# An attention and two-layer MoE kernel: w_in fetched up front, GpSimd without elementwise work behind the gating, column maxima turned at later steps

## The chip, the cores and the metric

One core of one Trainium2 chip runs the kernel. The metric is the device time of one execution in microseconds (us); the time given for a kernel is the median of its runs.

## The reference

The inputs are q, k, v of shape (4, 8, 576, 64), s of shape (4, 8, 576), and for each of two layers w_in (512 x 2048) and w_out (2048 x 512) in float64. Cut to what matters:

```
scores = q @ k^T / sqrt(64) + min(cum_k - cum_q, 0)   # causal; cum = cumsum(max(s, 0))
x  = softmax(scores) @ v                # 4 x 8 x 576 x 64 -> 2304 tokens x 512
h  = x @ w1_in;  g = h * tanh(log(1 + exp(h)));       x = g @ w1_out
h2 = x @ w2_in;  g2 = h2 * sigmoid(1.702 * h2);     out = g2 @ w2_out
```

## The kernel before

**Stages.** Attention runs over 4 batches, 8 heads and blocks of 128 rows (576 is 4.5 blocks). The first layer's first matmul runs between its steps, for units of 256 tokens: `first_layer` makes `h` out of `xh` (x, split in a high and a low part) and a tile `w` of w_in, and stores it to DRAM (`h_d`). Then the *gating* (`act`) loads pieces `hg` of it, applies Mish on ScalarE (`z`) and splits the result into `gh` (high) and `gl` (low). The second matmul of the first layer (`acc<-gh,w`, `acc<-gl,w`) goes over 5 *spans* of tokens, four of 512 and one of 256, with 16 *steps* each; a step is one block of 128 rows of w_out and has 12 matmuls. The accumulators `acc` of a span of 512 tokens hold four PSUM banks, and spans use two sets of four in turn. After a span, `out1` copies the banks out, takes maxima (`mx`) and stores x to DRAM (`x_d`). The second layer makes `h` out of x in fp16 halves (`x16`) and `w2i` (`first2`), `z<-h,sg` behind a sigmoid, combinations `s` of its four quarters (`combos`), and `p<-w2h,gl` and the like with seven products in place of eight (`second2`). Every product of split numbers is three matmuls: high by high, high by low, low by high (`mm3`).

**Weights.** They arrive as float64. `fetch_w` loads a piece as 128x1024 int32 (512 KB) into a tile `wst`; `turn_w` converts it: a scaling on ScalarE, a shift (TENSOR_SCALAR) and one or two SCALAR_TENSOR_TENSOR of 128x512 on VectorE, then the high half `th` and the low half `tl_`. In the first layer's w_out, both halves are made on GpSimd. w_in has 16 pieces, `fetch_a` fetches them in order from a list `fq`, and `bg_a` turns the next; `first_layer` calls both as it goes. A dependency lets a fetch start only behind the last transpose of the opening (`weights behind transposes`).

**The second layer's weights** are scaled first, during the first layer's second matmul, as *jobs*, one at a step: `out_pass1` (16 times) converts a piece of w2_out, takes its maxima (`wom`) and stores it, `in_pass` (16 times) converts a piece of w2_in and takes `wim`, `in_split` makes `w2i`. `out_pass2` then reads w2_out back in pairs (`w2f`), makes four differences `w2d` of 128x256 on GpSimd, and splits them into `w2h` and `w2l`.

**Maxima across partitions.** `across(col, then, wait)` copies a column to 128x128 (`bc`) on VectorE; after `wait` calls of `soon_step`, one to a step and one at each end of a span, TensorE transposes it into a bank of the set not in use (`acc<-ident,bc`), and VectorE reduces it (`spx<-acc` or `gsc<-acc`). Seven columns go this way: the scale of w2_out (`out_scale`, wait 14), of w2_in (`in_scale`, wait 7), and the maximum of x in each of the five spans (wait 14 for the first three; the last two are taken at the second layer's start).

**Order.** The Tile framework's scheduler places instructions on the engines' queues by priority and dependencies; in the opening (`nc.mode = "strict"`) every engine keeps the order in which the program emits. The w_in pieces of the first layer and `h_d` go by SP's queue, q and k of later blocks by GpSimd's (`load_group`, `k_load`), with a doubling copy of each on ScalarE. All instructions are recorded at one line (L77, in `Lane.run`), so tiles' names tell them apart.

Of the kernel before, what the change touches and what calls it, by code (L numbers as in the profile page):

```python
# [29 lines left out]
SOON = 7  # L30
# [4 lines left out]
PTB = 5  # L35
WAH = 1
LAG0 = 2
NEAR = 26
FA = 3
XH = 3  # L40
# [50 lines left out]
def attention_moe_moe_kernel(  # L91
# [107 lines left out]

    def k_load(i, g):  # L200
        t = pp.tile([128, HG, 2, D], F32, tag="kraw", name="kraw", bufs=3)
        nc.gpsimd.dma_start(out=t[:, :, 0, :], in_=rows(k, 0, i, g))
        held(nc.scalar.activation(out=t[:, :, 1, :], in_=t[:, :, 0, :], func=AF.Copy))
        raw[0, i, g] = t

    def load_group(b, i, g):
        n = min(128, S - 128 * i)
        r = []
        for src, nm in ((k, "kraw"), (q, "qraw"), (v, "vraw")):
            if nm == "vraw" and b == 0:  # L210
                v_load(i, g, nc.gpsimd)
                continue
            w = 1 if nm == "vraw" else 2
            t = pp.tile([128, HG, w, D], F32, tag=nm, name=nm, bufs=2 if nm == "qraw" else 3)
            held(nc.gpsimd.dma_start(out=t[:n, :, 0, :], in_=rows(src, b, i, g)))
            if w == 2:
                held(nc.scalar.activation(out=t[:n, :, 1, :], in_=t[:n, :, 0, :], func=AF.Copy))
            else:
                t = t[:, :, 0, :]
            r.append(t)  # L220
        raw[b, i, g] = r
# [525 lines left out]
    def fetch_w(stage, lay, m, kind):  # L747
        if stage:
            rt = stage.tile([128, 1024], F32, tag="wst", name="wst", bufs=NRAW)
        else:  # L750
            rt = tmp_pair(F32, "wst")
        if wide:
            rv = rt.bitcast(I32)
            r = rv.rearrange("p (f two) -> p f two", two=2)
            src = (w1_in, w2_in, w1_out, w2_out)[lay + 2 * (kind == "out")].bitcast(I32)
        else:
            rv = r = rt[:, 0:DM]
            src = (w1_in, w2_in, w1_out, w2_out)[lay + 2 * (kind == "out")]
        if kind == "in":
            n = src.shape[1] // NF  # L760
            ld = nc.sync.dma_start(
                out=rv.rearrange("p (c f) -> p c f", c=KC),
                in_=src[:, m * n:(m + 1) * n].rearrange("(c p) f -> p c f", p=128),
            )
            if lay == 0 and last_pt[0] is not None:
                tc.add_manual_dep(ld.ins, last_pt[0].ins.name, order, reason="weights behind transposes")
        else:
            nc.sync.dma_start(out=rv, in_=src[m * 128:(m + 1) * 128, :])
        fetched[lay, m, kind] = r

    def turn_w(pool, lay, m, kind):
# [19 lines left out]
        if not sided:  # L791
            nc.vector.scalar_tensor_tensor(
                out=yi, in0=yi, scalar=-(2 ** 31), in1=zi, op0=ALU.bitwise_and, op1=ALU.bitwise_or
            )
        if lay == 0 and kind == "out":
            nc.gpsimd.tensor_scalar(out=th, in0=y, scalar1=1.0, scalar2=0.0, op0=ALU.mult, op1=ALU.add)
        else:
            nc.scalar.activation(out=th, in_=y, func=AF.Copy)
        nc.gpsimd.tensor_tensor(out=tl_, in0=y, in1=th, op=ALU.subtract)

# [187 lines left out]
    def act(i):  # L988
# [5 lines left out]
        for e in range(2):  # L994
# [61 lines left out]
    def across(col, then, wait=SOON):  # L1056
# [150 lines left out]
    def out_pass2(j):  # L1207
# [19 lines left out]
    for i, (u, t0, W, m0, n) in enumerate(groups1):  # L1227
# [24 lines left out]
        if m0 + n == NF:  # L1252
# [3 lines left out]
            def out1(e, acc=acc, k_=k_, mx=mx, u=u, t0=t0, W=W):  # L1256
# [167 lines left out]
```

## Time and profile before

| | |
|---|---|
| median of 3 runs | 1035.53 us (1034.38 to 1039.54) |
| profiled execution | 1039.73 us, of which the span is 1038.0 |
| mean granted clock of TensorE | 0.978 |
| busy: TensorE | 985.0 us (95%) |
| busy: VectorE | 689.9 us (66%) |
| busy: ScalarE | 544.9 us (52%) |
| busy: GpSimd | 387.2 us (37%) |
| DMA | 143.17 MB, mean 138 GB/s |

The shares of busy time are means over stages. In the page's slices of 25.95 us, VectorE has nine tenths or eight in those from 415 to 571 us, and three to six tenths in the last quarter; TensorE has nine tenths in nearly all. The granted clock is a share of 2.4 GHz: 0.50 is the lower level, 1.2 GHz. In the rows below, PE is TensorE, DVE VectorE, ACT ScalarE, POOL GpSimd. A row of a timeline gives start and duration in us, engine, operation, out<-in, count, and in brackets the idle time before it and what ended that. A row of waits gives who waited for whom, the total, how often, and the longest. A row of windows gives a stretch, its length, each engine's busy time (x instructions), the granted clock, the share of the DMA engines and GB/s. A row of groups gives the shape, the count, busy us in total, the mean of one in ns, and the idle time before them with what ended it.

### The profile page before, as it was taken

How to read it: one execution, taken by the hardware profiler on the slowest of the kernel's cores; microseconds unless marked ns; L12 is line 12 of the kernel's file. 1: busy time of each engine (PE TensorE's matmuls, PEld its weight loads, DVE VectorE, ACT ScalarE, POOL GpSimd, SP SyncE). 2: the span in 40 equal slices, each digit the busy share in tenths (PEclk: the TensorE clock that was granted, in tenths of full speed). 3: DMA queues.
4: the chain of work that ended last, by engine and by line, in shares of the span. 5: the costliest groups of instructions: out<-in, count | busy, mean ns of one | idle time of the engine just before them, and what ended most of it. 6: DMA issues, size and time to landing. Idle time of an engine off the chain costs nothing.

```text
span 1038.0 us, 20212 instructions
## 1 busy us (share of the span) xinstructions
PE 985.0 (95%) x7966; PEld 872.4 (84%) x7970; DVE 689.9 (66%) x1257; ACT 544.9 (52%) x1054; POOL 387.2 (37%) x414
## 2 busy tenths in 40 slices
PE   6799999989989899999996989999999999999997
PEld 5688798879979789998885868988888888888886
DVE  6478677755565775799998984985653653653553
ACT  4476577766665885365655564553433433333331
POOL 2544442243123311586321315575343442342431
PEclk9789999999999999999998999999999999999999
DMA  6458359997699978779996552600110100000000
GB/s 174 107 146 246 102 133 167 221 234 164 138 212 220 171 158 182 271 268 347 339 339 211 201 203 81 203 22 1 41 42 1 39 24 1 21 19 3 21 9 34
DMA packets 153775, 143.17 MB, mean 138 GB/s; under 512 B 91216, under 2 KB 122448, under 8 KB 153680
## 3 DMA queue, kind: packets, MB, share of 16 engines
q1 hardware_dynamic: 147456, 124.05, 43.9%
q0 software_dynamic: 6224, 17.83, 6.7%
q8 instruction: 62, 1.02, 0.4%
q14 instruction: 33, 0.27, 0.1%
HBM read 89.61 MB, written 32.58 MB: 118 GB/s over the span
## 4 chain that ended last, share of the span: by engine, by line
PE 48%; DVE 11%; DMA 10%; issue 3%; ACT 3%; POOL 2%; SPq 1%; DVEq 0%; ACTq 0%; POOLq 0%
PE h L77 24%; PE p L77 16%; DVE wst L77 5%; PE acc L77 4%; PE s L77 2%; DMA wst<-in_moe_w_out_dram 2%; DMA pt<-hl 2%; PE o L77 1%; DMA wst<-in_moe_w_in_dram 1%; DVE gl L77 1%; DMA vraw<-in_v_dram 1%; DMA h_d<-hs 1%; POOL w L77 1%; POOL w2d L77 1%; DMA w2f<-w_d 1%
## 5 line engine op out<-in xcount | busy, mean ns | idle before, releaser
L77 PE MATMUL h<-x,w2i 128*128 128x256 f16 x1728 | 200.0, 273 | 0.0
L77 PE MATMUL acc<-gh,w 128*128 128x512 f32 (+1 forms) x640 | 185.0, 374 | 13.5 <-DVE spx L77 13.5
L77 PE MATMUL h<-xh,w 128*128 128x256 f32 x1344 | 196.6, 295 | 1.1 <-ACT xh L77 0.7
L77 PEld LDWEIGHTS <-w2i 128*128 128x128 f16 x1728 | 169.0, 98 | 19.6
L77 PEld LDWEIGHTS h<-xh,w 128*128 128x128 f32 x1344 | 172.8, 195 | 4.1 <-ACT xh L77 1.1
L77 PEld LDWEIGHTS acc<-gh,w 128*128 128x128 f32 x640 | 117.9, 191 | 35.8 <-DVE spx L77 14.4
L77 PE MATMUL p<-w2h,gl 128*128 128x256 f16 x504 | 135.9, 273 | 1.1 <-DVE gl L77 1.1
L77 PE MATMUL p<-w2l,gh 128*128 128x256 f16 x504 | 136.0, 273 | 0.0
L77 PE MATMUL p<-w2h,gh 128*128 128x256 f16 x504 | 133.4, 273 | 1.1 <-ACT gh L77 0.9
L77 POOL TENSOR_TENSOR s<-z 128x256 f32<-128x256 f32 x72 | 54.7, 780 | 201.8 <-DVE z L77 201.8
L77 PE MATMUL acc<-gl,w 128*128 128x512 f32 (+1 forms) x320 | 119.2, 373 | 0.0
L77 PEld LDWEIGHTS <-gh 128*128 128x128 f16 x1008 | 98.5, 98 | 12.9 <-ACT gh L77 1.2
L77 ACT ACTIVATE sg<-h,spx 128x512 f32<-128x512 f32 x72 | 48.7, 680 | 105.0 <-PE h L77 105.0
L77 DVE TENSOR_TENSOR gl<-z,gh 128x768 f16<-128x768 f32 (+1 forms) x54 | 77.1, 1428 | 34.5 <-ACT gh L77 21.9
L77 DVE SCALAR_TENSOR_TENSOR wst<-wst 128x512 int32<-128x512 int32 x96 | 91.1, 958 | 10.0 <-ACT wst L77 6.6
L77 DVE SCALAR_TENSOR_TENSOR z<-h,sg 128x512 f32<-128x512 f32 x72 | 49.3, 687 | 68.8 <-ACT sg L77 68.7
L77 POOL TENSOR_TENSOR gl<-z,gh 128x1024 fp32r<-128x1024 f32 x18 | 51.0, 2832 | 116.9 <-ACT gh L77 103.8
L77 DVE TENSOR_TENSOR gl<-s,gh 128x1024 f16<-128x1024 f32 x36 | 44.2, 1228 | 68.5 <-ACT gh L77 68.5
L77 ACT ACTIVATE gh<-z 128x1024 fp32r<-128x1024 f32 (+1 forms) x72 | 67.9, 947 | 33.8 <-DVE z L77 29.4
L77 PE MATMUL s<-kw,qw 128*128 128x288 f32 (+4 forms) x352 | 81.8, 339 | 2.4 <-DVE kw L77 2.2
L77 ACT ACTIVATE gh<-s 128x1024 f16<-128x1024 f32 x36 | 38.0, 1057 | 81.7 <-POOL s L77 81.7
L77 ACT ACTIVATE P<-P,mx 128x128 f32<-128x128 f32 (+4 forms) x108 | 62.7, 582 | 19.9 <-DVE mx L77 19.5
(146 smaller groups left out, 1765.2 us busy)
## 6 DMA issues: line engine op xcount, KB each, us to landing
h_d<-hs SPq DMA_DIRECT2D x36, 512.0 KB, 4.4
hg<-h_d SPq DMA_DIRECT2D x36, 512.0 KB, 6.4
wst<-in_moe_w_in_dram SPq DMA_DIRECT2D x32, 512.0 KB, 5.3
wst<-in_moe_w_out_dram SPq DMA_DIRECT2D x32, 512.0 KB, 5.4
ck<-cum_d SPq DMA_DIRECT2D x6, 768.0 KB, 7.8
x_d<-x SPq DMA_DIRECT2D x18, 256.0 KB, 5.2
out_dram<-o SPq DMA_DIRECT2D x9, 512.0 KB, 2.8
kraw<-in_k_dram POOLq DMA_DIRECT2D x32, 128.0 KB, 4.1
```

What stands on the lines that cost most here:

```text
L77: r = f(*a, **kw)
```

## The change

(1) All 16 pieces of w_in are fetched in the opening, into slots of the pool that holds their converted form (the last into a slot of another pool); the dependency behind the transposes is gone, and `first_layer` fetches no more. `load_group` and `k_load` of the third block of rows are issued earlier, without their doubling copies, which follow later (`twice`). `bg_a` is called more often in the opening, and `WAH` goes from 1 to 3. (2) `act` makes both `gl` on VectorE; the low half of w_out is made on VectorE and the high half on ScalarE; the differences `w2d` are made on VectorE. GpSimd keeps the low halves of w_in and `combos`. (3) `across` counts absolute steps where `wait` is over 7: 57 for `out_scale`, 66 for `in_scale`, and 59, 60, 65, 999, 999 for the five spans.

```diff
-WAH = 1
+WAH = 3
...
-FA = 3
...
+    def twice(t, n=128):
+        held(nc.scalar.activation(out=t[:n, :, 1, :], in_=t[:n, :, 0, :], func=AF.Copy))
...
-            rt = tmp_pair(F32, "wst")
+            rt = (wa_p if m < NF - 1 else mo_a).tile([128, 1024], F32, tag="w" if m < NF - 1 else "hs", name="wst")
...
-            if lay == 0 and last_pt[0] is not None:
-                tc.add_manual_dep(ld.ins, last_pt[0].ins.name, order, reason="weights behind transposes")
...
-        if lay == 0 and kind == "out":
-            nc.gpsimd.tensor_scalar(out=th, in0=y, scalar1=1.0, scalar2=0.0, op0=ALU.mult, op1=ALU.add)
-        else:
-            nc.scalar.activation(out=th, in_=y, func=AF.Copy)
-        nc.gpsimd.tensor_tensor(out=tl_, in0=y, in1=th, op=ALU.subtract)
+        nc.scalar.activation(out=th, in_=y, func=AF.Copy)
+        (nc.gpsimd if kind == "in" else nc.vector).tensor_tensor(out=tl_, in0=y, in1=th, op=ALU.subtract)
...
-    for _ in range(FA):
+    while fq:
         fetch_a()
...
     score(3)
+    load_group(0, 2, 0, False)
+    for i_ in range(2):
+        k_load(i_, 0, False)
...
-    load_group(0, 2, 0)
-    for i_ in range(2):
-        k_load(i_, 0)
+    for t in raw[0, 2, 0][0:2] + [raw[0, 0, 0], raw[0, 1, 0]]:
+        twice(t)
+    bg_a()
+    bg_a()
...
-    pop_prep(len(prep_q))
+    while prep_q:
+        pop_prep(1)
+        bg_a()
...
-            (nc.vector if e == 0 else nc.gpsimd).tensor_tensor(out=gl[e], in0=z, in1=gh[e], op=ALU.subtract)
+            nc.vector.tensor_tensor(out=gl[e], in0=z, in1=gh[e], op=ALU.subtract)
...
-        soon.append([wait, turn])
+        soon.append([wait - (clock[0] if wait > SOON else 0), turn])
+
+    clock = [0]
 
     def soon_step():
+        clock[0] += 1
...
-        across(gsc[:, 0:1], out_scale2, 2 * SOON)
+        across(gsc[:, 0:1], out_scale2, 57)
...
-        across(gsc[:, 2:3], in_scale2)
+        across(gsc[:, 2:3], in_scale2, 66)
...
-        sub = lambda o, a, b_: nc.gpsimd.tensor_tensor(out=o, in0=a, in1=b_, op=ALU.subtract)
+        sub = lambda o, a, b_: nc.vector.tensor_tensor(out=o, in0=a, in1=b_, op=ALU.subtract)
...
-                        spx[:, u, 0:1], lambda: span_scale(u) if ready[0] else waiting.append(u), 2 * SOON if u < 3 else 99
+                        spx[:, u, 0:1], lambda: span_scale(u) if ready[0] else waiting.append(u), (59, 60, 65, 999, 999)[u]
```

The order of instructions moves at three places. The first is TensorE in the opening, up to the third score of 384 columns (`s<-kw,qw`; the number behind a name tells tiles apart). Before:

```order
L77 MATMUL h<-xh,w 128x256 x36
L77 MATMUL kt<-ident,kraw 128x128 x8
L77 MATMUL qt<-ident,qraw 128x128 x4
L77 MATMUL kt<-ident,kraw 128x128 x4
L77 MATMUL s<-kw_442,qw 128x384 x2
L77 LDWEIGHTS oneh
L77 MATMUL s<-cumb,oneh 128x384
L77 LDWEIGHTS identb
L77 MATMUL s<-maskb,identb 128x128
L77 MATMUL kt<-ident,kraw 128x128 x8
L77 MATMUL pt<-ident,P 128x128 x4
```

And now:

```order
L76 MATMUL h<-xh,w 128x256 x38
L76 MATMUL kt<-ident,kraw 128x128 x8
L76 MATMUL qt<-ident,qraw 128x128 x4
L76 MATMUL kt<-ident,kraw 128x128 x4
L76 MATMUL h<-xh,w 128x256 x22
L76 MATMUL s<-kw_480,qw 128x384 x2
L76 LDWEIGHTS oneh
L76 MATMUL s<-cumb,oneh 128x384
L76 LDWEIGHTS identb
L76 MATMUL s<-maskb,identb 128x128
L76 MATMUL h<-xh,w 128x256 x14
L76 MATMUL kt<-ident,kraw 128x128 x8
```

By that score TensorE has 60 matmuls of the first layer behind it in this piece where it had 36, and 14 more stand behind the mask, ahead of the next transposes of k.

The second is VectorE around the reductions of turned maxima (`spx<-acc`, `gsc<-acc`). Before, the one of the second span stands among the last of w2_in's conversions:

```order
L77 TENSOR_REDUCE rk<-wim 128x1
L77 TENSOR_SCALAR rk<-rk 128x1
L77 RECIPROCAL rk<-rk 128x1
L77 TENSOR_SCALAR rk<-rk 128x1
L77 RECIPROCAL rk<-rk 128x1
L77 TENSOR_REDUCE mx_7265<-x_7266 128x1
L77 SCALAR_TENSOR_TENSOR w2i<-wst,rk,w2i 128x512 x2
L77 TENSOR_REDUCE spx<-acc 128x1
L77 SCALAR_TENSOR_TENSOR w2i<-wst,rk,w2i 128x512 x2
L77 TENSOR_REDUCE mx_7265<-x_7270 128x1
L77 TENSOR_REDUCE mx_7265<-x_7332 128x1
```

Now the first three turned maxima (`gsc<-acc`, then two `spx<-acc`) follow the first scalings `w2i<-wst`; the first of the three stands three rows ahead of these, and the copies `bc` of the columns stand beside them:

```order
L76 SCALAR_TENSOR_TENSOR w2i<-wst,rk,w2i 128x512
L76 RECIPROCAL gsc<-gsc 128x1
L76 SCALAR_TENSOR_TENSOR w2i<-wst,rk,w2i 128x512
L76 TENSOR_SCALAR gsc<-gsc 128x1
L76 SCALAR_TENSOR_TENSOR w2i<-wst,rk,w2i 128x512
L76 RECIPROCAL gsc<-gsc 128x1
L76 TENSOR_TENSOR gl<-z,gh 128x1024
L76 TENSOR_SCALAR gsc<-gsc 128x1
L76 COPY bc<-spx 128x128
L76 TENSOR_REDUCE spx<-acc 128x1
L76 COPY bc<-gsc 128x128
L76 TENSOR_REDUCE spx<-acc 128x1
```

The reductions of the maxima now come one upon another, behind all of w2_in's conversions.

The third is VectorE where the second layer starts, from the last maximum of the fourth span (`spx<-mx`) to the third `z`. Before:

```order
L77 TENSOR_REDUCE mx_8297<-x_8298 128x2
L77 TENSOR_REDUCE mx_8297<-x_8302 128x2
L77 TENSOR_REDUCE spx<-mx_8297 128x1
L77 COPY bc<-spx 128x128
L77 SCALAR_TENSOR_TENSOR w2l<-w2d,gsc,w2h 128x1024
L77 SCALAR_TENSOR_TENSOR z_8350<-h_8352,sg 128x512
L77 SCALAR_TENSOR_TENSOR z_8350<-h_8379,sg 128x512
L77 TENSOR_TENSOR gl_8412<-z_8350,gh_8411 128x2x384
L77 SCALAR_TENSOR_TENSOR z_8449<-h_8451,sg 128x512
```

And now:

```order
L76 SCALAR_TENSOR_TENSOR z_8350<-h_8352,sg 128x512
L76 TENSOR_TENSOR w2d<-w2f 128x256 x2
L76 COPY bc<-spx 128x128
L76 SCALAR_TENSOR_TENSOR w2l<-w2d,gsc,w2h 128x1024
L76 TENSOR_TENSOR w2d<-w2f,w2d 128x256
L76 SCALAR_TENSOR_TENSOR w2l<-w2d,gsc,w2h 128x1024 x2
L76 TENSOR_TENSOR w2d<-w2f 128x256 x2
L76 TENSOR_TENSOR w2d<-w2d,w2f 128x256
L76 SCALAR_TENSOR_TENSOR w2l<-w2f,gsc,w2h 128x256
L76 SCALAR_TENSOR_TENSOR z_8350<-h_8379,sg 128x512
L76 SCALAR_TENSOR_TENSOR w2l<-w2f,gsc,w2h 128x512
L76 SCALAR_TENSOR_TENSOR z_8449<-h_8451,sg 128x512
```

The differences `w2d`, which GpSimd made before, and the low halves `w2l` that follow from them stand between the `z`.

## Rows read from the trace of the kernel before

**Rows 1.** Timeline of TensorE (PE), 458 to 702 us

```profile
458.68 0.40 PE L77 MATMUL acc<-gh,w 128*128 128x512 f32 x1
...
546.01 0.27 PE L77 MATMUL acc<-ident,bc 128*128 128x128 f32 x1
...
561.16 0.79 PE L77 MATMUL acc<-gh,w 128*128 128x512 f32 x1 [9.63 <-DVE spx L77]
...
613.44 0.65 PE L77 MATMUL acc<-gh,w 128*128 128x512 f32 x1 [3.92 <-DVE spx L77]
...
651.83 0.27 PE L77 MATMUL acc<-ident,bc 128*128 128x128 f32 x1
...
674.87 10.65 PE L77 MATMUL h<-x,w2i 128*128 128x256 f16 x96
```

**Rows 2.** Waits of TensorE, 410 to 700 us

```profile
PE acc L77 <- DVE spx L77: 13.5, 2, 9.6
PE p L77 <- DVE gl L77: 1.1, 1, 1.1
PE p L77 <- ACT gh L77: 0.9, 1, 0.9
```

**Rows 3.** Windows from 420 to 700 us

```profile
502.00:546.00 44.00, 44.00 (x195) 36.29 (x194) 42.70 (x61) 26.43 (x34) 11.81 (x4) 1.00 0.98 349
...
sum 280.00, PE 264.49 PEld 228.77 DVE 246.39 ACT 159.31 POOL 130.91; mean PE 37.78 PEld 32.68 DVE 35.20 ACT 22.76 POOL 18.70
```

**Rows 4.** Windows of three stretches with a low clock

```profile
51.00:57.00 6.00, 5.44 (x25) 4.96 (x26) 3.53 (x6) 4.21 (x10) 2.88 (x4) 0.50 0.16 46
561.00:565.00 4.00, 3.84 (x9) 3.07 (x10) 2.98 (x6) 1.72 (x4) 0.00 (x0) 0.50 0.80 227
613.00:617.00 4.00, 3.56 (x9) 2.79 (x10) 4.00 (x5) 3.84 (x5) 3.13 (x2) 0.58 1.05 364
```

**Rows 5.** Timeline of VectorE (DVE) and GpSimd (POOL), 587 to 593 us

```profile
587.10 0.42 DVE L77 TENSOR_SCALAR wst<-wst 128x512 int32<-128x512 int32 x1
...
588.11 1.20 DVE L77 TENSOR_TENSOR gl<-z,gh 128x1024 fp32r<-128x1024 f32 x1
...
588.78 2.79 POOL L77 TENSOR_TENSOR gl<-z,gh 128x1024 fp32r<-128x1024 f32 x1 [2.74 <-DVE gsc L77]
...
589.24 2.62 DVE L77 TENSOR_SCALAR wst<-wst 128x512 int32<-128x512 int32 x1
...
592.37 0.14 DVE L77 TENSOR_SCALAR gsc<-gsc 128x1 f32<-128x1 f32 x1
...
592.43 0.68 DVE L77 SCALAR_TENSOR_TENSOR wst<-wst 128x512 int32<-128x512 int32 x1
```

**Rows 6.** VectorE's groups by shape, 415 to 690 us

```profile
L77 DVE SCALAR_TENSOR_TENSOR wst<-wst 128x512 int32<-128x512 int32 x80 | 79.4, 1004 | 5.6 <-ACT wst L77 2.9 <-DVE wst L77 0.5
L77 DVE TENSOR_SCALAR wst<-wst 128x512 int32<-128x512 int32 x48 | 37.6, 784 | 9.1 <-DMA wst<-in_moe_w_out_dram 4.6 <-DMA wst<-in_moe_w_in_dram 4.5
L77 DVE TENSOR_TENSOR gl<-z,gh 128x1024 fp32r<-128x1024 f32 x18 | 26.3, 1464 | 13.6 <-PE acc L77 12.6 <-ACT gh L77 1.0
...
L77 DVE TENSOR_REDUCE wom<-w2y 128x1 f32<-128x512 f32 x16 | 10.9, 682 | 0.3
```

**Rows 7.** VectorE's groups by shape, 0 to 415 us

```profile
L77 DVE TENSOR_TENSOR xh<-xt,xh 128x256 fp32r<-128x256 f32 x11 | 4.6, 419 | 0.1
```

**Rows 8.** GpSimd's groups by shape, 415 to 700 us

```profile
L77 POOL TENSOR_TENSOR gl<-z,gh 128x1024 fp32r<-128x1024 f32 x18 | 51.0, 2832 | 116.9 <-ACT gh L77 103.8 <-issue 6.3 <-DMA hg<-h_d 4.0
```

**Rows 9.** Timeline of TensorE, 0 to 62 us

```profile
48.75 0.62 PE L77 MATMUL s<-kw,qw 128*128 128x384 f32 x2 [2.16 <-DVE kw L77]
...
51.56 1.97 PE L77 MATMUL kt<-ident,kraw 128*128 128x128 f32 x8 [1.96 <-ACT kraw L77]
```

**Rows 10.** The chain that ended last, 640 to 700 us

```profile
650.61 6.11 DMA x_d<-x
```

**Rows 11.** Timeline of VectorE, 683 us

```profile
683.37 1.28 DVE L77 SCALAR_TENSOR_TENSOR z<-h,sg 128x512 f32<-128x512 f32 x2
```

More of the change, by code (lines that the diff above doesn't have):

```diff
@@ L198, in v_load, with k_load, load_group @@
         return eng.dma_start(out=t[:n], in_=rows(v, 0, i, g))
-    def k_load(i, g):
+    def twice(t, n=128):
+        held(nc.scalar.activation(out=t[:n, :, 1, :], in_=t[:n, :, 0, :], func=AF.Copy))
+    def k_load(i, g, dup=True):
         t = pp.tile([128, HG, 2, D], F32, tag="kraw", name="kraw", bufs=3)
         nc.gpsimd.dma_start(out=t[:, :, 0, :], in_=rows(k, 0, i, g))
-        held(nc.scalar.activation(out=t[:, :, 1, :], in_=t[:, :, 0, :], func=AF.Copy))
         raw[0, i, g] = t
-    def load_group(b, i, g):
+        if dup:
+            twice(t)
+    def load_group(b, i, g, dup=True):
         n = min(128, S - 128 * i)
@@ L215, in load_group @@
             held(nc.gpsimd.dma_start(out=t[:n, :, 0, :], in_=rows(src, b, i, g)))
-            if w == 2:
-                held(nc.scalar.activation(out=t[:n, :, 1, :], in_=t[:n, :, 0, :], func=AF.Copy))
-            else:
+            if w == 1:
                 t = t[:, :, 0, :]
+            elif dup:
+                twice(t, n)
             r.append(t)
@@ L760, in fetch_w @@
             n = src.shape[1] // NF
-            ld = nc.sync.dma_start(
+            nc.sync.dma_start(
                 out=rv.rearrange("p (c f) -> p c f", c=KC),
@@ L794, in turn_w @@
             )
-        if lay == 0 and kind == "out":
-            nc.gpsimd.tensor_scalar(out=th, in0=y, scalar1=1.0, scalar2=0.0, op0=ALU.mult, op1=ALU.add)
-        else:
-            nc.scalar.activation(out=th, in_=y, func=AF.Copy)
-        nc.gpsimd.tensor_tensor(out=tl_, in0=y, in1=th, op=ALU.subtract)
+        nc.scalar.activation(out=th, in_=y, func=AF.Copy)
+        (nc.gpsimd if kind == "in" else nc.vector).tensor_tensor(out=tl_, in0=y, in1=th, op=ALU.subtract)
     def mm3(outp, hi_w, lo_w, hi_x, lo_x, start, stop):
@@ L825, in bg_a @@
             m = wq.pop(0)
-            while fq and fq[0] <= m:
-                fetch_a()
             turn_w(wa_p, 0, m, "in")
@@ L889, in attention_moe_moe_kernel @@
     nxt[0] = avn[0] = 6
-    load_group(0, 2, 0)
-    for i_ in range(2):
-        k_load(i_, 0)
+    for t in raw[0, 2, 0][0:2] + [raw[0, 0, 0], raw[0, 1, 0]]:
+        twice(t)
+    bg_a()
+    bg_a()
     nc.gpsimd.memset(maskp, 0.0)
@@ L928, in first_layer @@
                         bg_a()
-                    while fq and fq[0] <= m + 2 * e + d + WAH + FA:
-                        fetch_a()
                     l1_mm(ps[:, d * U:(d + 1) * U], 0, m + 2 * e + d, xr, d == 0)
```

## The prediction

> **What bounds the kernel now.** I read the waits of TensorE first, then its timeline, then the windows, then VectorE's and GpSimd's groups. The program has three stages. Up to 415 us attention runs with the first matmul of the first layer between its steps. From 415 to 674.87 the first layer is finished and its second matmul runs; the rows give its bounds: the first gated matmul at 458.68, the end of the fourth span of 512 tokens at 651.83, the first matmul of the second layer at 674.87 [rows 1]. From there to the end TensorE is busy in every window but for some 2 us, so the last stage is a fixed length that merely starts earlier or later.
>
> The waits say where TensorE stood still: 13.5 us in two waits for VectorE's `spx`, and 1.1 us more for `gl` [rows 2]. The timeline places them: 9.63 us before 561.16 and 3.92 us before 613.44 [rows 1]. Both follow a transposed maximum: the transpose at 546.01 fills a PSUM bank that the next span needs, and VectorE reads it only some 15 us later, because the read stands behind other work in its queue. VectorE is that late because it is full: 42.70 of the 44 us from 502 to 546, and 246.39 of the 280 us from 420 to 700 [rows 3]. Each wait also leaves TensorE slow: 4 us after the first at a granted clock of 0.50, 4 us after the second at 0.58 [rows 4]. The lower level is 1.2 of 2.4 GHz, so those cost 2.0 and 1.7 us more.
>
> Why VectorE is full is the main reading. An unhindered scalar_tensor_tensor of 128x512 takes 0.68 us, a shift (TENSOR_SCALAR) 0.42, a `gl` subtraction of 128x1024 1.20; the shift that meets GpSimd's `gl` (588.78, 2.79 us long) takes 2.62 us and ends as that ends [rows 5]. Over the stage the means are 1004, 784 and 1464 ns, while the reductions, which read one operand, stay at 682 [rows 6]. So a good part of VectorE's busy time is standing behind GpSimd.
>
> **The change, part by part.** *Work moved off GpSimd behind gating.* VectorE gets 18 `gl` at 1.20, 16 low halves of w_out at 0.68 and 32 differences of 128x256 at 0.42 [rows 5, 7]: 21.6 + 10.9 + 13.4 = 45.9 us more. It gets back what those rows were stretched by: 80 x (1004 - 680) = 25.9, 48 x (784 - 420) = 17.5, 18 x (1464 - 1200) = 4.8, together 48.2 us, and something on smaller groups. VectorE is thus about as full as before, but evenly, and GpSimd's 2832 ns per `gl` [rows 8] leave the way to the second matmul. The bounds are 0 and 48.2 us back; I take the upper end, since the collision is in the rows. ScalarE gets 16 more conversions; it is far from full, and eight banks of accumulators cover it.
>
> *Maxima late.* The order puts the five transposes after steps 54, 56, 57.8, 62 and 64 of the gated matmul (a step is 12 matmuls, 2.75 us by the rows: 193.15 us less the 17.2 lost, over 64 [rows 1]); before, they stood at 32, 39, 48, 61 and 64. None is now at a change of spans that needs its bank: the span of 256 tokens uses others. Between two of them VectorE has 4.9 to 11 us to read the bank, with VectorE waiting for TensorE rather than the reverse. What goes is both waits with their slow clock: 13.5 + 2.0 + 1.7 = 17.2 us. If VectorE still came late by a step, up to 4 us would stay; at best 17.2 go.
>
> *w_in up front.* All 16 loads stand on SP's queue behind v, so nothing needed earlier is passed; SP issued nine of them over 51 us, held by slots, and now only issues. GpSimd's loads of k and q for the third block of 128 rows start when their slots come free, well before 40 us, and share the queues with w_in. In the order TensorE gets 22, 14 and 12 first-layer matmuls where it waited 2.16 us for `kw` and 1.96 us for `kraw` [rows 9], and the 6 us from 51 to 57, with 5.44 us of matmuls at 0.50 [rows 4], should run at full clock: 2.7 us. That is 6.8 us at most. But the matmuls are only brought forward: by the third score of 384 columns 86 are used instead of 48, and the scores behind have fewer between them. How much that gives back is in no row; between 0 and all of it. I take 5.0, nearer the upper end, since the rest of the 192 matmuls of that unit of 256 tokens still stands between the steps behind.
>
> *The hand-over to the second layer* pays. Behind the last maximum's reduction VectorE's order now holds, up to and with the second `z`: 35 small instructions (0.14), 18 differences and 8 subtractions of 128x256 (0.42), 17 instructions of 128x512 (0.68) and 6 of 128x1024 (1.20) [rows 5, 7]: 4.9 + 10.9 + 11.6 + 7.2 = 34.6 us. The 128x512 maxima of the fourth span wait in it too: their copy needs a slot that a 6.11 us store of x frees [rows 10], which I put at 2.5 us. So the second `z` comes some 37 us after the span's end. Before it came at 684.65, 33 us after [rows 11], and then the two `p` waits were 2.0 us together (the 1.1 of [rows 2] and 0.9 for `gh`). TensorE needs its bank 23.0 us (the last span) and 10.65 us (96 matmuls) behind that end [rows 1], at 33.7. The wait is 3.3 us, with the third `z` behind it about 5, and 2 us of slow clock: 7, less the 2.0 that goes: 5.0 us lost. It is 0 if VectorE's instructions overlap more than their durations say, 10 if loads of w2 come late as well.
>
> **Sum.** 17.2 + 5.0 - 5.0 = 17.2 us. The profiled execution took 1039.73 us, which would make it 1022.5; the median of the runs lies 4.2 us below it, at 1035.53, and against that I give **1018**.
>
> **The rivals.** (1) *VectorE becomes the bound*, slower than now. If its rows are long for a reason of their own, 45.9 us come on top of 246.39 in 280 [rows 3]: 292.3, so the stage grows by 12.3 us and takes the gain with it: 1035.5 + 12.3 - 5.0 = 1043. It decides if less than about 12 us come back. For it: VectorE is the fullest engine there. Against: the reductions keep their 682 ns, and the long shift ends with GpSimd's instruction. The Trainium skill, Perfetto Trace Analysis, section Optimizing Scalar/DVE Operations, says that with VectorE saturated, moving work to ScalarE or even GpSimd may make sense, and warns that between VectorE and GpSimd it might not help; the first half speaks for this rival, the second against, and the rows side with the second. 0.04.
>
> (2) *The waits for maxima come back at their new places.* Five transposes within ten steps use one bank; should VectorE be more than two steps late there, two waits like the 3.92 us one with their slow clock return, 2 x 5.6 = 11 us, and 1029 to 1033 is left. Against: VectorE has nothing left of w2_in to do then but the last four scalings. 0.07.
>
> (3) *The hand-over costs 10 us or more and the opening brings little*: 17.2 + 2 - 10, or 1026. For it: VectorE's queue there is a chain with ScalarE, stores and loads. 0.15.
>
> (4) *The change does not do what it says*: each converted w_in takes the slot of the one fetched before it, so conversions follow one another, and TensorE waits for them at 45 to 75 us. The opening then gives nothing: 1023, inside the forecast's own range. 0.10, counted with it.
>
> (5) *More than forecast*: no loss at the hand-over and the whole opening, 17.2 + 6.8 = 24: 1011. 0.08.
>
> **How the numbers follow.** The forecast, 1013 to 1024, has 0.66 with (4). About 0.5%, 5 us, is what a measurement of this kernel tells from no change. Faster by more: forecast, (3) and (5), 0.89; within it: (2), 0.07; slower: (1), 0.04. The range leaves out (1) and most of (2) and reaches from (5) with a little more opening to (3) with a little more loss: 1008 to 1029.
>
> **What would show it.** Right: no wait of TensorE for `spx` before 640 us; the span from the first gated matmul to the fourth span's end about 176 us instead of 193.15; scalar_tensor_tensor of 128x512 near 690 ns and shifts near 430; full clock from about 44 us on; one wait of 3 to 8 us some 10 us after the second layer's first matmul. Wrong: VectorE's means unchanged, a wait of TensorE for `gl` of the gating, or waits at the transposes 54 to 62.

## The result and the profile after

The changed kernel takes 1021.57 us (median of 5 runs, 1017.52 to 1023.25) where the kernel before takes 1036.53 (5 runs, the three of the table above among them): a ratio of 0.9842, interval 0.9820 to 0.9865. The profiled execution took 1023.25 us, 1021.2 of it the span. The forecast of 1018 and its range hold; two of its three terms don't.

The timeline of TensorE in the changed kernel, against [rows 1]:

```profile
460.95 0.40 PE L76 MATMUL acc<-gh,w 128*128 128x512 f32 x1
...
608.32 0.27 PE L76 MATMUL acc<-ident,bc 128*128 128x128 f32 x1
...
636.14 0.27 PE L76 MATMUL acc<-ident,bc 128*128 128x128 f32 x1
...
659.28 10.65 PE L76 MATMUL h<-x,w2i 128*128 128x256 f16 x96
...
670.31 0.33 PE L76 MATMUL h<-ident,bc 128*128 128x128 f32 x1 [0.26 <-DVE z L76]
671.57 5.40 PE L76 MATMUL h<-x,w2i 128*128 128x256 f16 x48 [0.93 <-DVE z L76]
```

From these rows the program has three stretches. Up to the first gated matmul: 458.68 us before, 460.95 now, 2.3 us *lost*. From there to the second layer's first matmul: 216.2 before, 198.3 now, 17.9 gained; there is no wait for `spx`. From there to the end: 363.1 before (1038.0 less 674.87), 361.9 now, 1.2 gained: the two waits for `p` [rows 2] are gone, and 0.93 + 0.26 us for `z` have come. 17.9 + 1.2 - 2.3 is the 16.8 us between the two spans. Each is read from one execution; the first gated matmul comes at 453.80 to 460.95 us over the profiles of this study, so the 2.3 us say little by themselves.

VectorE's groups by shape in the changed kernel, 415 to 690 us, against [rows 6]:

```profile
L76 DVE SCALAR_TENSOR_TENSOR wst<-wst 128x512 int32<-128x512 int32 x80 | 53.7, 686 | 1.9 <-ACT wst L76 1.4
L76 DVE TENSOR_TENSOR gl<-z,gh 128x1024 fp32r<-128x1024 f32 x36 | 43.8, 1219 | 6.1 <-ACT gh L76 5.5 <-DMA h_d<-hs 0.6
L76 DVE TENSOR_SCALAR wst<-wst 128x512 int32<-128x512 int32 x48 | 20.4, 425 | 18.1 <-DMA wst<-in_moe_w_out_dram 13.6 <-DMA wst<-in_moe_w_in_dram 4.4
...
L76 DVE TENSOR_REDUCE wom<-w2y 128x1 f32<-128x512 f32 x16 | 10.9, 682 | 0.2
```

The stretch is gone: 1004 to 686 ns, 784 to 425, 1464 to 1219, and the reductions stay at 682. Two windows of the changed kernel (length, busy us of PE, PEld, DVE, ACT, POOL, clock, DMA share, GB/s); the second goes from the first gated matmul to the end of the fourth span:

```profile
75.00:100.00 25.00, 22.54 (x157) 18.88 (x160) 19.71 (x38) 13.81 (x33) 11.26 (x10) 0.92 0.45 122
461.00:636.00 175.00, 175.00 (x773) 144.29 (x773) 145.06 (x256) 105.22 (x134) 1.55 (x2) 1.00 0.75 264
```

and the same of the kernel before:

```profile
75.00:100.00 25.00, 24.56 (x190) 21.39 (x193) 20.39 (x39) 17.23 (x39) 11.82 (x12) 1.00 0.77 238
458.68:652.00 193.32, 179.77 (x776) 147.14 (x775) 165.84 (x248) 108.70 (x138) 73.28 (x41) 0.96 0.71 245
```

VectorE is busy for 145.06 us where it was for 165.84, though it has more to do. The other pair of rows, 75 to 100 us, is for the opening, below.

### The profile page after: what moved, and what is told of

Read it like the earlier page. It is cut to its first block, busy times and chain, and to the rows that moved or that the text cites. A ratio compares the mean times of both kernels' runs of the same rounds, so it can differ in the third digit from the quotient of the medians.

```text
span 1021.2 us, 20117 instructions
## 1 busy us (share of the span) xinstructions
PE 981.8 (96%) x7967; PEld 870.5 (85%) x7970; DVE 668.9 (66%) x1323; ACT 552.7 (54%) x1070; POOL 269.4 (26%) x332
## 4 chain that ended last, share of the span: by engine, by line
PE 63%; DMA 2%; DVE 1%; ACT 0%; issue 0%; DVEq 0%; SPq 0%
PE acc L76 24%; PE h L76 21%; PE p L76 16%; DMA pt<-hl 2%; PE s L76 1%; PE o L76 1%; DVE w2l L76 0%; PE xt L76 0%; PE qt L76 0%; PE kt L76 0%; DVE z L76 0%; DVE w2d L76 0%; DVE o L76 0%; DVE f L76 0%; ACT P L76 0%
## 5 line engine op out<-in xcount | busy, mean ns | idle before, releaser
L76 PE MATMUL acc<-gh,w 128*128 128x512 f32 (+1 forms) x640 | 181.7, 369 | 0.0
L76 DVE TENSOR_TENSOR gl<-z,gh 128x1024 fp32r<-128x1024 f32 (+1 forms) x72 | 94.5, 1314 | 26.2 <-ACT gh L76 25.5
L76 DVE CUSTOM_DVE_ANT_0 P<-s,ck 128x128 f32<-128x128 f32 (+3 forms) x96 | 44.6, 486 | 38.1 <-PE s L76 31.1
L76 PEld LDWEIGHTS acc<-gl,w 128*128 128x128 f32 x320 | 60.4, 189 | 10.2
```

What stands on the lines that cost most here:

```text
L76: r = f(*a, **kw)
```

## The experiments

**Each part alone.** The change has three parts; each was put alone into the kernel before.

(1) Only w_in up front:

```diff
-    for _ in range(FA):
+    while fq:
         fetch_a()
...
+    load_group(0, 2, 0, False)
...
+    while prep_q:
+        pop_prep(1)
+        bg_a()
```

> Only w_in up front (with the earlier loads of k and q and the extra conversions); GpSimd and the maxima as in the kernel before. Theory A (the opening's gain is kept): about 5 us faster than before, 1031, with the first gated matmul near 453. Rival B (the matmuls that are brought forward are missing as filling behind the later scores, so the idle time and the slow clock only move from 44 to 57 us to the windows from 75 us on): 1034 to 1039, no gain, first gated matmul within 3 us of 459. The trace of the changed kernel, where it came at 461, speaks for B. The two waits for spx stay in either case, 13.5 us together or so.

1038.70 us, ratio 0.9994 (0.9973 to 1.0015): no gain, and the first gated matmul at 459.08. Rival B. Windows of this run, same columns:

```profile
44.00:51.00 7.00, 6.57 (x53) 5.95 (x52) 4.74 (x7) 5.00 (x11) 5.19 (x6) 1.00 0.40 119
51.00:57.00 6.00, 5.67 (x47) 4.97 (x46) 2.90 (x5) 4.54 (x12) 5.18 (x6) 1.00 0.21 64
75.00:100.00 25.00, 23.29 (x168) 19.37 (x167) 19.10 (x36) 13.60 (x33) 10.08 (x9) 0.93 0.45 122
```

The opening does what the prediction wanted: TensorE is busy for 12.24 of the 13 us from 44 to 57 at full clock, where [rows 4, 9] had waits and a granted clock of 0.50. From 75 to 100 us it then has 168 matmuls where the kernel before has 190, idles longer, and the granted clock is 0.93 instead of 1.00. Over all the profiles of this study the first gated matmul comes at 457.1 us on average with w_in as before (nine kernels, 455.57 to 458.68) and at 457.6 with w_in up front (five, 453.80 to 460.95). Nothing is kept. That the matmuls brought forward are missing as filling later fits these rows; it was not tested by itself.

(2) Only GpSimd's work moved, `gl`, w_out's halves and `w2d`:

```diff
-        if lay == 0 and kind == "out":
-            nc.gpsimd.tensor_scalar(out=th, in0=y, scalar1=1.0, scalar2=0.0, op0=ALU.mult, op1=ALU.add)
...
+            nc.vector.tensor_tensor(out=gl[e], in0=z, in1=gh[e], op=ALU.subtract)
...
+        sub = lambda o, a, b_: nc.vector.tensor_tensor(out=o, in0=a, in1=b_, op=ALU.subtract)
```

> Only the work moved off GpSimd; w_in and the maxima as before. Theory A (the gain comes from where the maxima are turned; VectorE gets as much stretch back as it takes over in work): about the time of before, 1033 to 1038, with waits of TensorE for spx of 8 to 16 us left. Rival C (the gain comes from VectorE getting free of GpSimd, so that it reads the turned maxima in time even at the old steps): 1018 to 1025, waits for spx under 4 us. Rival D (VectorE's rows are long for a reason of their own): 1045 or more. A and C expect scalar_tensor_tensor of 128x512 near 690 ns, D near 1000.

1020.61 us, ratio 0.9821 (0.9794 to 0.9848): the whole gain, from the part that the prediction gave nothing for, with the maxima at their old steps. Rival C. TensorE's first transpose in this run, and VectorE's read of it:

```profile
543.99 0.27 PE L77 MATMUL acc<-ident,bc 128*128 128x128 f32 x1
```

VectorE's timeline:

```profile
544.94 0.28 DVE L77 TENSOR_REDUCE spx<-acc 128x1 f32<-128x128 f32 x1
```

and the read in the kernel before, of the transpose at 546.01 [rows 1]:

```profile
560.82 0.28 DVE L77 TENSOR_REDUCE spx<-acc 128x1 f32<-128x128 f32 x1
```

14.8 us late before, 0.95 now, both at step 32. VectorE's main group in this run, 415 to 690 us as in [rows 6], has the short duration that was expected:

```profile
L77 DVE SCALAR_TENSOR_TENSOR wst<-wst 128x512 int32<-128x512 int32 x80 | 53.9, 684 | 2.1 <-ACT wst L77 1.5
```

(3) Only the maxima late:

```diff
-        across(gsc[:, 0:1], out_scale2, 2 * SOON)
+        across(gsc[:, 0:1], out_scale2, 57)
...
+                        spx[:, u, 0:1], lambda: span_scale(u) if ready[0] else waiting.append(u), (59, 60, 65, 999, 999)[u]
...
```

> Only the maxima turned at the new steps; GpSimd as before. Theory A: the 17 us come from this part, 1017 to 1022, no wait for spx. Rival C: VectorE, still stretched by GpSimd, is late at the new steps too: waits for spx (or gsc) of 4 us or more at steps 54 to 62, or waits for gl of the gating, and 1025 to 1034.

1036.77 us, ratio 0.9981 (0.9962 to 1.0): no gain that counts. TensorE's first two transposes in this run:

```profile
607.66 0.33 PE L77 MATMUL acc<-ident,bc 128*128 128x128 f32 x1 [1.71 <-ACT x L77]
...
622.32 0.47 PE L77 MATMUL acc<-ident,bc 128*128 128x128 f32 x1 [8.88 <-DVE gsc L77]
```

and VectorE's read of the first:

```profile
621.99 0.28 DVE L77 TENSOR_REDUCE gsc<-acc 128x1 f32<-128x128 f32 x1
```

VectorE reads the first one 14.3 us late here too, and since the transposes share a bank, the second one waits 8.9 us for that. The waits went from `spx` at the changes of spans to `gsc` at the new steps: rival (2) of the prediction. The waits are those that rival C expected; the time is above its range too.

**In pairs.** (4) The moved work and the late maxima, w_in as before. Against (2):

```diff
...
-        across(gsc[:, 2:3], in_scale2)
+        across(gsc[:, 2:3], in_scale2, 66)
...
-                        spx[:, u, 0:1], lambda: span_scale(u) if ready[0] else waiting.append(u), 2 * SOON if u < 3 else 99
+                        spx[:, u, 0:1], lambda: span_scale(u) if ready[0] else waiting.append(u), (59, 60, 65, 999, 999)[u]
```

> The work moved off GpSimd and the maxima late, w_in as before. Theory A on the opening (5 us kept): 3 to 6 us slower than the whole change, 1025 to 1027. Rival B on the opening (nothing kept): the time of the whole change or a little below, 1017 to 1022.

1023.28 us, 1.3 above rival B's range and 1.7 below theory A's. The ratio of 0.9855 (0.9828 to 0.9881) lies within the whole change's interval, which speaks for B: w_in as before costs nothing that shows. Beside (2) on the same chip it is slower, 1022.90 to 1025.11 against 1018.70 to 1021.67. The stretch up to the second layer is the same in both profiles (198.3 us), the last stage is longer, 365.8 against 362.0. Where, says the second layer's start (GpSimd, ScalarE, TensorE):

```profile
662.89 3.97 POOL L77 TENSOR_TENSOR s<-z 128x256 f32<-128x256 f32 x2 [10.13 <-DVE z L77]
...
669.17 1.06 ACT L77 ACTIVATE gh<-s 128x1024 f16<-128x1024 f32 x1 [5.04 <-POOL s L77]
...
670.28 0.28 PE L77 MATMUL p<-w2h,gh 128*128 128x256 f16 x1 [3.64 <-ACT gh L77]
```

GpSimd's first two `s` take some 2 us each, against a mean of 1.05 for the 14 of that kind from 655 to 720 us of this run; ScalarE waits for GpSimd (5.04 us), TensorE for ScalarE (3.64). VectorE is full there (8.00 of the 8 us from 662 to 670): in this run it splits x for the second layer until 651.7 us, in (2) only until 636.1.

(5) The whole change with GpSimd's work put back:

```diff
-            nc.vector.tensor_tensor(out=gl[e], in0=z, in1=gh[e], op=ALU.subtract)
+            (nc.vector if e == 0 else nc.gpsimd).tensor_tensor(out=gl[e], in0=z, in1=gh[e], op=ALU.subtract)
```

and the same for w_out and `w2d`.

> The whole change with GpSimd's work put back: w_in up front and the maxima at the new steps alone. Theory E (all of the gain hangs on VectorE not being late): the gain goes, 1031 to 1038, with a wait of 5 us or more for one of the turned maxima, since five transposes share a bank and VectorE reads some 10 to 15 us late. Rival (the two other parts do together what neither does alone): 1018 to 1026, no such wait.

1038.66 us, just above theory E's range, ratio 1.0006 (0.998 to 1.0032). Its second transpose waits 7.54 us for `gsc`. All of the gain hangs on GpSimd.

(6) w_in up front and GpSimd's work moved, maxima at the old steps. Against the whole change:

```diff
-        across(gsc[:, 0:1], out_scale2, 57)
+        across(gsc[:, 0:1], out_scale2, 2 * SOON)
...
-        across(gsc[:, 2:3], in_scale2, 66)
+        across(gsc[:, 2:3], in_scale2)
...
```

> w_in up front and the work moved off GpSimd, maxima at the old steps. Theory E (the maxima's new steps add nothing once VectorE is less than 5 us late): the changed kernel's time, 1018 to 1024, no wait for spx over 1 us. Rival (the new steps are needed): waits for spx of 3 us or more, 1027 or later.

1015.97 us, 2 us below theory E's range, ratio 0.9796 (0.9767 to 0.9826): the fastest kernel of the study. The interval touches the changed kernel's (0.9820 to 0.9865), so the lead over it is likely, not certain. TensorE at the start of its second layer:

```profile
656.03 10.65 PE L76 MATMUL h<-x,w2i 128*128 128x256 f16 x96
...
667.18 2.78 PE L76 MATMUL h<-x,w2i 128*128 128x256 f16 x24
```

ScalarE's first scaling of x for the second layer in this run:

```profile
629.41 2.56 ACT L76 ACTIVATE x<-x,spx 128x512 f16<-128x512 f32 x4 [6.49 <-DVE spx L76]
```

and in the changed kernel:

```profile
640.30 2.55 ACT L76 ACTIVATE x<-x,spx 128x512 f16<-128x512 f32 x4
```

There is no wait between the first two of its matmul groups, and the last stage is 360.3 us. The scaling of x begins 10.9 us later in the changed kernel (7.6 us when both are counted from their first gated matmul), since `span_scale` runs only once w2_in's scale is there, and that is turned last. In these runs late maxima squeeze the hand-over and give nothing for it.

**What on GpSimd does it.** (7) Only the 18 `gl` moved:

```diff
-            (nc.vector if e == 0 else nc.gpsimd).tensor_tensor(out=gl[e], in0=z, in1=gh[e], op=ALU.subtract)
+            nc.vector.tensor_tensor(out=gl[e], in0=z, in1=gh[e], op=ALU.subtract)
```

> The kernel before with one thing moved: the 18 gl that GpSimd made are made on VectorE; w_out's halves and the differences w2d stay on GpSimd. Theory E (GpSimd's instructions stretch VectorE's that meet them, VectorE falls behind, and so reads the first turned maximum late): gl is 51 of some 92 us that GpSimd spends on gl and w_out, so a part of the gain, by shares of the stretch 48 x 51/92 = 27 us back against 21.6 us added: waits for spx of 3 to 12 us left, 1022 to 1033, scalar_tensor_tensor of 128x512 between 750 and 900 ns. Rival F (what counts is that a gl of 2.8 us on GpSimd makes its operands late for TensorE and its slots late for ScalarE): the whole gain, 1018 to 1022.

(8) Only w_out's halves moved:

```diff
-            nc.gpsimd.tensor_scalar(out=th, in0=y, scalar1=1.0, scalar2=0.0, op0=ALU.mult, op1=ALU.add)
...
+        (nc.gpsimd if kind == "in" else nc.vector).tensor_tensor(out=tl_, in0=y, in1=th, op=ALU.subtract)
```

> The kernel before with the two halves of w_out moved off GpSimd (high to ScalarE, low to VectorE); gl and w2d stay on GpSimd. Theory E: w_out is 41 of some 92 us, and runs before 502 us, where VectorE's backlog is built: 10.9 us added, some 21 back, a part of the gain, 1022 to 1033 with waits for spx of 3 to 12 us. Rival F: no gain, 1034 to 1040, waits of 13 us left.

(7) takes 1021.60 us, ratio 0.9852 (0.9822 to 0.9882), (8) 1034.56, ratio 0.9972 (0.995 to 0.9993). By the time alone rival F would be right, and E's times are missed: it divided the gain by shares of the stretch. The rows tell otherwise. TensorE waits for no `gl` of the gating in the kernel before [rows 2]. VectorE's groups in (7):

```profile
L77 DVE SCALAR_TENSOR_TENSOR wst<-wst 128x512 int32<-128x512 int32 x80 | 67.8, 859 | 2.5 <-ACT wst L77 0.6
```

and its timeline in (7):

```profile
547.13 0.28 DVE L77 TENSOR_REDUCE spx<-acc 128x1 f32<-128x128 f32 x1
```

The same group in (8):

```profile
L77 DVE SCALAR_TENSOR_TENSOR wst<-wst 128x512 int32<-128x512 int32 x80 | 68.5, 869 | 5.4 <-ACT wst L77 4.5
```

and VectorE's timeline in (8):

```profile
556.61 0.28 DVE L77 TENSOR_REDUCE spx<-acc 128x1 f32<-128x128 f32 x1
```

Either one takes back a little under half of the stretch, 859 and 869 ns of 1004, with 684 to 686 left when all is moved. But (7) reads the transpose of 542.90 at 547.13, 4.2 us late, and (8) that of 544.75 at 556.61, 11.9 late and with a wait of 6.69. From 502 to 562 us `gl` is all that GpSimd does in the kernel before. Windows from 78 us ahead of the first gated matmul to the read (same columns as above), of the kernel before:

```profile
380.68:560.82 180.14, 170.27 (x1134) 150.16 (x1132) 152.65 (x209) 100.81 (x152) 77.64 (x52) 0.99 0.86 275
```

of (7):

```profile
377.57:547.13 169.56, 169.09 (x1130) 149.53 (x1129) 144.74 (x221) 101.16 (x152) 47.78 (x41) 1.00 0.91 292
```

and of (8):

```profile
379.42:556.61 177.19, 169.98 (x1131) 149.88 (x1130) 141.28 (x224) 110.36 (x166) 35.50 (x20) 1.00 0.88 279
```

VectorE's shifts in (8), in that stretch:

```profile
L77 DVE TENSOR_SCALAR wst<-wst 128x512 int32<-128x512 int32 x36 | 22.0, 612 | 12.1 <-DMA wst<-in_moe_w_out_dram 12.1
```

(8) takes more busy time off VectorE ahead of the read than (7), 11.4 us against 7.9. But VectorE's idle time (length less busy time) grows by 8.4 us in (8), most of it waits for loads of w_out, 12.1 us against 4.6 in the kernel before; in (7) it shrinks by 2.7. So the read comes 2.9 us sooner in (8) and 10.6 in (7): time that was returned ahead of those loads went into the waits for them.

F has a small share. A `gl` on GpSimd also holds the slot that ScalarE's next `z` needs. ScalarE in the kernel before:

```profile
554.13 1.06 ACT L77 ACTIVATE z<-hg 128x1024 f32<-128x1024 f32 x1 [2.74 <-POOL gl L77]
```

and VectorE:

```profile
555.76 1.42 DVE L77 SCALAR_TENSOR_TENSOR wst<-wst 128x512 int32<-128x512 int32 x2 [1.38 <-ACT wst L77]
```

VectorE waits 1.38 us for a conversion that stood behind this `z`, 5 us ahead of the read: about a tenth of its lateness.

(9), (10) Is it the meeting of the two engines, or GpSimd being slow with something that is needed? The kernel of (2), and on GpSimd three instructions with each second `gl`, whose result nobody reads:

```diff
             nc.vector.tensor_tensor(out=gl[e], in0=z, in1=gh[e], op=ALU.subtract)
+            if e:
+                scrap = mb.tile([128, 256], F32, tag="scrap", name="scrap")
+                for o in range(0, 768, 256):
+                    nc.gpsimd.tensor_tensor(out=scrap, in0=z[:, o:o + 256], in1=gh[e][:, o:o + 256], op=ALU.subtract)
```

and in (10) the last line with one operand:

```diff
+                    nc.gpsimd.tensor_scalar(out=scrap, in0=z[:, o:o + 256], scalar1=1.0, scalar2=0.0, op0=ALU.mult, op1=ALU.add)
```

> The kernel of the run with only GpSimd's work moved, and on GpSimd 54 subtractions of 128x256 with two operands in SBUF (three where each gl stood), whose result nobody reads. Theory E: VectorE's rows are stretched again, scalar_tensor_tensor of 128x512 at 800 ns or more, and since VectorE keeps the moved work as well, waits of TensorE for spx or gl come back: 1030 to 1050. Rival F: nobody waits for these, so the time stays at 1018 to 1024 and the rows at 690.

> The same with 54 copies of 128x256 with one operand (tensor_scalar) in place of the subtractions. If the collision needs two operands on GpSimd's side: rows near 690, 1018 to 1024. If any pass of GpSimd through SBUF stretches VectorE: as with the subtractions, by the share of their busy time, 1025 to 1045.

(9) takes 1031.59 us, ratio 0.9947 (0.9915 to 0.9978), 11 us more than (2); (10) takes 1021.70, ratio 0.9857 (0.9829 to 0.9885). VectorE's group in (9):

```profile
L77 DVE SCALAR_TENSOR_TENSOR wst<-wst 128x512 int32<-128x512 int32 x80 | 59.9, 760 | 1.5 <-ACT wst L77 0.9
```

GpSimd's group in (9):

```profile
L77 POOL TENSOR_TENSOR scrap<-z,gh 128x256 f32<-128x256 f32 x54 | 64.1, 1188 | 157.7 <-ACT gh L77 154.9
```

VectorE's first read in (9), of a transpose at 544.58:

```profile
553.17 0.28 DVE L77 TENSOR_REDUCE spx<-acc 128x1 f32<-128x128 f32 x1
```

The same three in (10), VectorE's group:

```profile
L77 DVE SCALAR_TENSOR_TENSOR wst<-wst 128x512 int32<-128x512 int32 x80 | 55.9, 710 | 1.6 <-ACT wst L77 0.9
```

GpSimd's group:

```profile
L77 POOL TENSOR_SCALAR scrap<-z 128x256 f32<-128x256 f32 x54 | 38.3, 709 | 170.8 <-ACT z L77 167.7
```

and the first read, of a transpose at 543.66:

```profile
549.58 0.28 DVE L77 TENSOR_REDUCE spx<-acc 128x1 f32<-128x128 f32 x1
```

Instructions whose result nobody reads bring the waits back. They are not quite without a waiter: like a `gl` on GpSimd, the subtractions hold the slot of their operand, and ScalarE waits for it, 14.9 us in eight waits, the longest 4 us ahead of the read:

```profile
549.09 1.06 ACT L77 ACTIVATE z<-hg 128x1024 f32<-128x1024 f32 x1 [4.01 <-POOL scrap L77]
```

But this does not reach VectorE: it waits for nothing from 530 us to its read. Counted as in (7) and (8), its busy time up to the read is 12.6 us longer than in (2) (143.79 against 131.19) and its idle time 5.0 shorter; that is the 7.6 us by which its read comes later. So it is the meeting. The rows came to 760 ns, not the 800 expected. In (10) no engine waits for the copies. With one operand GpSimd is busy for 38.3 us instead of 64.1 and stretches VectorE's rows only to 710; a part of the 5.9 us of lateness there is a wait of VectorE for a store of `w2y`, 3.3 us against 0.4 in (2). The two forms differ in length as well (709 and 1188 ns), so what the second operand does and what the shorter time does isn't separated.

The Trainium skill (SBUF — State Buffer, section Who interferes with whom) says that VectorE and GpSimd share a pair of ports as an exclusive lock, that VectorE's instructions with two operands in SBUF and its tensor_scalar in a fast mode are drawn into it, and tensor_reduce on trn2 never is. The groups agree: 1004 against 686 ns, 784 against 425, and the reductions at 682 in both. That whoever comes second stands still for the whole instruction fits the shift that ends with GpSimd's `gl` [rows 5]. The page makes no difference between GpSimd's forms as long as they read SBUF; here the copies stretched VectorE's rows by 26 ns (684 to 710) for 38.3 us of GpSimd, the subtractions by 76 for 64.1, so for each us the copies did a little over half as much.

**How late is too late.** The same first transpose, step 32, in six kernels; the bank is needed two steps later:

| kernel | first read behind its transpose | TensorE's wait there | first gated matmul to second layer |
|---|---|---|---|
| before | 14.8 us | 9.63 | 216.2 |
| (8) w_out moved | 11.9 | 6.69 | 213.5 |
| (9) idle subtractions | 8.6 | 3.19 | 207.2 |
| (10) idle copies | 5.9 | 0.52 | 203.2 |
| (7) gl moved | 4.2 | 0 | 198.4 |
| (2) all moved | 0.95 | 0 | 198.3 |

The wait is the lateness less 5.2 to 5.4 us in every row that has one. The transpose at step 48 shows the same with more room: read 10.9 us late before, 11.0 in (8), 9.2 in (9), 9.0 in (10), TensorE waits 3.92, 3.98, 2.46 and 2.19 us, the lateness less 6.8 to 7.0. Below the room VectorE's lateness costs TensorE nothing there, which is why (7) has the whole gain with over half of the stretch left. At step 48 it has it narrowly: its read is 6.6 us late.

(11) The same from the other side, in the kernel before:

```diff
-                        spx[:, u, 0:1], lambda: span_scale(u) if ready[0] else waiting.append(u), 2 * SOON if u < 3 else 99
+                        spx[:, u, 0:1], lambda: span_scale(u) if ready[0] else waiting.append(u), 2 * SOON + 4 if u < 3 else 99
```

> The kernel before with one number changed: the first three spans' maxima wait 18 steps in place of 14, so that the two transposes that TensorE waited behind stand 3 steps past a change of spans (35 and 51 in place of 32 and 48), and their bank is needed 13 steps later (some 36 us) in place of 2 (5.4 us). GpSimd keeps all its work, VectorE stays some 15 us late. Theory E2 (what TensorE loses is VectorE's lateness less the time until the bank is needed, and nothing else of the stretch costs): both waits go, 1018 to 1023, with scalar_tensor_tensor still near 1000 ns. Rival (a VectorE that is late holds TensorE up at the next thing: gl of the gating, w2i, another maximum): waits of 5 us or more elsewhere, 1027 to 1038.

1033.34 us, ratio 0.9953 (0.993 to 0.9977), a quarter to a third of the changed kernel's gain. TensorE's first two transposes in this run:

```profile
553.15 0.33 PE L77 MATMUL acc<-ident,bc 128*128 128x128 f32 x1 [0.72 <-ACT x L77]
...
569.19 0.48 PE L77 MATMUL acc<-ident,bc 128*128 128x128 f32 x1 [4.81 <-DVE spx L77]
```

and VectorE's read of the first:

```profile
568.85 0.28 DVE L77 TENSOR_REDUCE spx<-acc 128x1 f32<-128x128 f32 x1
```

Both old waits are gone, but the read comes 15.7 us late, and the next maximum, due some 11 us behind the first, shares its bank: 4.81 us. The stretch to the second layer falls from 216.2 to 207.9 us, and 2.3 us of waits for `z`, with a granted clock of 0.57 from 680 to 684 us behind them, lengthen the last stage to 366.9. A late engine finds the next thing to hold up; here the rival was half right: its time came, its waits nearly.

(12) The whole change with the differences `w2d` left on GpSimd:

```diff
-        sub = lambda o, a, b_: nc.vector.tensor_tensor(out=o, in0=a, in1=b_, op=ALU.subtract)
+        sub = lambda o, a, b_: nc.gpsimd.tensor_tensor(out=o, in0=a, in1=b_, op=ALU.subtract)
```

> The whole change, but the 32 differences w2d stay on GpSimd. The prediction's term (the differences on VectorE cost about 5 us at the hand-over to the second layer): 1014 to 1018, last stage shorter than the changed kernel's 361.9 us. Rival (VectorE had room for them; the hand-over is bound by the same chain either way): 1019 to 1024, last stage 361 to 364 us.

1022.71 us, ratio 0.9876 (0.9847 to 0.9904): no gain from it. The time is the rival's; the last stage is neither's. It is *longer* than the changed kernel's, 367.4 us (1019.5 less 652.15):

```profile
664.58 0.33 PE L76 MATMUL h<-ident,bc 128*128 128x128 f32 x1 [1.78 <-DVE z L76]
...
668.74 7.46 PE L76 MATMUL h<-x,w2i 128*128 128x256 f16 x48
```

GpSimd takes 7.04 us for two of the differences from 642.80 us on; ScalarE waits up to 4.1 us for them, VectorE up to 3.2 us for ScalarE, and `z` comes late. 48 matmuls take 7.46 us where the changed kernel's took 5.40: behind the waits, the clock had fallen. Windows of 4 us from 666.15 and 670.15 show it granted at 0.50 and 0.65, and at 1.00 in the changed kernel.

## Why the prediction was right, and where it wasn't

**The bound.** Right: TensorE stood behind two turned maxima because VectorE was late, and VectorE was late because of GpSimd ((2), (9)). Both waits with their slow clock were put at 17.2 us; the stretch gained 17.9, and from the first gated matmul to the fourth span's end it takes 175.2 us where 176 was forecast.

**Which part removes them.** Wrong. The step that failed is *Maxima late*: "None is now at a change of spans that needs its bank", and VectorE would have "4.9 to 11 us to read the bank, with VectorE waiting for TensorE rather than the reverse". Alone, that part gains nothing (3), with w_in nothing (5), and beside the moved work it costs some 3 us ((4) against (2)). VectorE's lateness was some 14 us, more than the room at the new steps.

**The moved work.** The stretch was sized well (48.2 us forecast; at the durations of after it is 80 x 318, 48 x 359 and 18 x 245 ns, 47.1). The step that failed is the balance: 45.9 us added against 48.2 returned, over the whole stage, so "about as full as before" and a gain of nothing. What decides is the balance *ahead of the first critical read*, less what of it goes into waits for loads. VectorE's groups of the kernel before, 380 to 546 us:

```profile
L77 DVE SCALAR_TENSOR_TENSOR wst<-wst 128x512 int32<-128x512 int32 x50 | 55.8, 1123 | 2.8 <-DVE wst L77 0.5 <-ACT wst L77 0.2
L77 DVE TENSOR_SCALAR wst<-wst 128x512 int32<-128x512 int32 x34 | 26.7, 784 | 4.6 <-DMA wst<-in_moe_w_out_dram 4.6
L77 DVE TENSOR_TENSOR gl<-z,gh 128x1024 fp32r<-128x1024 f32 x10 | 15.4, 1539 | 1.0 <-ACT gh L77 1.0
L77 DVE SCALAR_TENSOR_TENSOR w2y<-wst 128x512 int32<-128x512 int32 x16 | 14.1, 884 | 0.0
```

and GpSimd's:

```profile
L77 POOL TENSOR_TENSOR gl<-z,gh 128x1024 fp32r<-128x1024 f32 x10 | 28.9, 2887 | 42.2 <-ACT gh L77 38.2 <-DMA hg<-h_d 4.0
```

With the unhindered durations (0.685, 0.425, 1.22, 0.685 us) those return 50 x 0.438 + 34 x 0.359 + 10 x 0.319 + 16 x 0.199 = 40.5 us. Added by then are only the ten `gl` and the 16 low halves of w_out, 12.2 + 11.0 = 23.2: the other `gl` and all the differences come later, when the room is there. 17.3 us net by this count. Counted up to the read itself, from 78 us ahead of the first gated matmul as in (7) and (8), VectorE's busy time falls by 21.5 us in (2) (152.65 to 131.19) and its idle time grows by 7.6, with 14.9 us of waits for loads of w_out where there were 4.6. The difference is the 13.9 us by which the read comes sooner (14.8 to 0.95 us behind its transpose).

**The opening.** Wrong: 5.0 us was put down, nothing came. The row of 51 to 57 us did turn to full clock, and the prediction named the doubt ("How much that gives back is in no row"); it chose the wrong end.

**The hand-over.** Wrong in size: 5.0 us of loss were forecast, 1.2 us were gained. The second `z` ends at 670.25 (0.68 us from 669.57), 34.1 us behind the fourth span's end at 636.14, not 37; the bank was needed at 33.8. The 2.5 us for a store of x did not show: VectorE is busy for 22.66 of the 23 us from 636 to 659. So the wait was 1.2 us and the clock did not fall. The two errors, 7.3 us too much at the opening and 6.2 too little here, cancel by luck, and the total came out nearer than its terms.

**The rivals.** (1) did not happen. (2) is what happens with GpSimd's work left in place. Of (3) one half came, the opening that brings little, and not the other. (4) and (5) did not happen; the time of (4) is near, but TensorE waited only 0.44 us for a converted w_in from 45 to 75 us.

## What to carry to other kernels

When an engine is late, ask by how much at the very instruction that is waited for, and against how much room; the loss is the difference, and anything that brings the lateness below the room buys all of it. Moving the wait elsewhere leaves the lateness, which finds the next shared buffer. Elementwise work on GpSimd also costs VectorE where the two meet, so move first what they meet in ahead of the critical read, and count what the late engine would then wait for: here 18 `gl` were enough, narrowly, and the 32 halves of w_out were not, for their time went largely into waits for loads.

## What was not expected of the hardware

64.1 us of subtractions on GpSimd whose result nobody reads cost 11 us of the program's time; 38.3 us of copies with one operand cost 1 by the medians, which is within the noise (their profile has 2.7 us of waits for `spx`). GpSimd's instructions vary as well: the idle subtractions, all of one form, took 732 to 3414 ns, 1188 on the mean. That VectorE slows them is likely, not shown. And 1.2 us of waits at the hand-over left the granted clock at 1.00, while 3.64 us in (4) and 3.4 us in (12) were followed by windows of 4 us at 0.72 (from 669.33 us) and 0.50, so that these waits cost more than their length.
